# Four layers on one core: the last 96 GLU columns as a 192-column product with a DMA transpose, in place of key features paired by sign

## The chip, the cores and the metric

The kernel runs on one core of a Trainium2 chip. The metric is the device time of one execution in microseconds; three runs of the kernel before gave a median of 396.29 us (395.6 to 396.61). The core has five engines that run side by side, each through its own list of instructions in order: TensorE (PE: matmuls, with a separate weight load), VectorE (DVE), ScalarE (ACT), GpSimd (POOL) and SyncE (SP, which here only issues DMAs). Matmuls write to PSUM, eight banks of 128 partitions by 512 floats; everything else lives in SBUF, 128 partitions wide.

## The reference

The input is x, 2048 tokens by 512, in bf16. Four residual layers follow, A, B, A, B, with the same weights for both A and for both B:

```
x = x + A(layernorm(x));  x = x + B(layernorm(x));  twice

A: q, k, v = x @ wqkv                       # 32 heads of 16
   pq, pk  = q @ w_phi, k @ w_phi           # a 16x16 matrix for each head
   phi_q   = [softmax(pq), softmax(-pq)]    # 32 features for each head
   phi_k   = [softmax(pk), softmax(-pk)]
   kv = sum_s phi_k[s]^T v[s];  z = sum_s phi_k[s]
   o  = (phi_q kv) / (phi_q z + 1e-6);  return o @ wo

B: h = relu(x @ W_gate) * (x @ W_up)        # 512 -> 1376
   return h @ W_down                        # 1376 -> 512
```

A is linear attention: one pass over all tokens sums the 16 x 16 matrices kv of each head and sign, a second pass applies them. B is a gated unit whose inner width is 1376 = 10 x 128 + 96.

## The kernel before, in words

All weights and all activations stay in SBUF. The 2048 tokens are 16 tiles of 128, and four tiles make a slab of 512. `x_sb` holds tokens on partitions; after each layer norm (`ln`) the tile is transposed by a DMA (issued by SP, `dma_tr`, L393) into `yT`, with features on partitions, as the matmuls want it.

**Layer A, keys and values.** `kv_proj` (one tile) and `kv_pair` (two tiles) project a tile to pk and v in PSUM. w_phi is folded into the weights beforehand (`compose_k`, `compose_q`). ACT takes exp(pk) and exp(-pk) to `expk` and copies v to `vsb`, DVE sums each head's 16 features (`Zk`) and takes reciprocals (`rZk`), POOL multiplies (`phik`, L640; for the last two tiles half of it is DVE's). Then `kv_acc` (L662) adds the tile to the running sum in PSUM with eight matmuls, one for each of eight groups. In this version a group is four heads with both signs: 4 x 2 x 16 = 128 features as weights against 64 columns of v and one column of ones, 65 columns in all. The sums fill two banks, 0 and 1. When the last tile is in, `kv_fin` (L671) copies them to `kvbd`, masked so that each head keeps its own block, in two signs by two halves: four copies (L678) and four denominators (L683) on 64 partitions each, on DVE.

**Layer A, queries.** `q_proj` (L688) projects a slab and takes the exponentials (`expq`). `num` (L700) multiplies a tile's eight feature groups with `kvbd`: eight matmuls of 144 columns (L710), in three banks' worth of groups. Then come the normalization on DVE and POOL, a DMA transpose to `oT`, the product with wo (L741) and the residual (L743).

**Layer B.** `glu_up` (L747) goes through the 11 chunks of the inner width for a slab, or for a piece of two tiles (the first slab is cut into two such pieces). For each chunk it makes four matmuls for gate and four for up with the weights stationary and the slab's tokens as 512 (or 256) columns (L762), into two PSUM banks from a ring of four. ACT takes the relu of gate (L764); for the chunks in `on_act` ACT also copies up to a scratch in `expk` (L770) and DVE multiplies from SBUF (L772), otherwise DVE multiplies from PSUM (L775). The result, hidden units on partitions, goes to one of 18 units of `hT`. The last chunk is 96 wide and comes last. `glu_down` (L781) takes 11 matmuls for each tile (L790) and adds to x (L792).

**The order of work.** `emit` (L802) lists operations layer by layer, mixing the chunks of B with the numerators of the same layer pair and the keys of the next layer. Each operation carries a planned duration. `Program.schedule` then makes the order of each engine itself: it derives the dependences from the resources that each operation reads and writes (a PSUM bank, a tile, an hT unit), and searches by list scheduling forwards and backwards with the planned durations, keeping the order with the shortest planned span. So a changed duration or dependence can move any instruction. Within an engine the order is then fixed, waits included. In layer 0 the first slab's queries are projected early, through a ring of two banks, 2 and 3 (`qr0`, L811); bank 3 also serves `compose_q`.

## Time and profile before

| what | value |
|---|---|
| median of three runs | 396.29 us |
| profiled execution | 396.61 us, span 394.9 us |
| PE | 376.9 us busy (95% of the span), 2331 matmuls |
| DVE | 271.8 us busy (69%) |
| ACT | 205.7 us busy (52%) |
| POOL | 173.3 us busy (44%) |
| gate and up products (L762) | 880 matmuls, 259.0 us busy by the modelled ends |
| key-value accumulation (L666) | 256 matmuls of 65 columns, 12.7 us busy |
| granted PE clock, mean | 0.991 |

The span runs from the first to the last instruction of the program; the profiled execution's own time is 1.7 us longer. Busy time of PE is counted with modelled ends of the matmuls, which overlap in the pipeline, so a mean duration (193 ns for 65 columns, 379 ns for 512) says how long one takes from start to result, and not how far apart two of them start. In the view of slices each digit stands for one fortieth of the span, about 9.9 us, in tenths.

The stages in time: to about 56 us layer 0's keys and values, to about 75 us the first numerators of layer 0, to 225 us layers 0 and 1 mixed and the first keys of layer 2, to 246 us the rest of layer 2's keys and the accumulation, to 262 us its first numerators, and then layers 2 and 3 mixed, to the end.

### The profile page before, as it was taken

What the parts mean: (1) busy time and instruction counts of PE and PEld (TensorE: products, weight loads), DVE (VectorE), ACT (ScalarE), POOL (GpSimd) and SP (SyncE); (2) the same over time, 40 slices, a digit from 0 to 9 for tenths busy, and PEclk for the clock granted to TensorE, in tenths of its full rate; (3) what the DMA queues carried; (4) which work ended last, traced back from release to release, by engine and by line L of the source; (5) the groups of instructions that cost most, each with busy time, mean ns of one, the idle gap of its engine ahead of it and who ended that gap; (6) DMA issues with size and microseconds to landing.
All of it is one profiled execution on the core that took longest, in us unless ns stands there. A gap on an engine that the chain in (4) does not pass through costs nothing.

```text
span 394.9 us, 6391 instructions
## 1 busy us (share of the span) xinstructions
PE 376.9 (95%) x2331; PEld 202.0 (51%) x2331; DVE 271.8 (69%) x551; ACT 205.7 (52%) x389; POOL 173.3 (44%) x286
## 2 busy tenths in 40 slices
PE   5897979899999999999999998899999999999997
PEld 4443435576844544444444454457774454444444
DVE  4999677896756888867766856897886675422222
ACT  5987768743634303542354375985563652553340
POOL 6499833751633373364243643385464352100000
PEclk9999889999999999999999999999999999999999
DMA  6833681322311223300100020133232113100002
GB/s 191 224 62 48 180 316 27 68 53 42 54 27 40 42 41 68 69 12 15 27 13 2 13 42 2 27 72 69 49 68 55 40 28 80 28 14 13 17 24 66
DMA packets 61663, 23.01 MB, mean 58 GB/s; under 512 B 53472, under 2 KB 60608, under 8 KB 61632
## 3 DMA queue, kind: packets, MB, share of 16 engines
q1 hardware_dynamic: 60912, 22.02, 24.1%
q10 hardware_dynamic: 720, 0.59, 0.5%
q8 instruction: 18, 0.29, 0.3%
q14 instruction: 13, 0.11, 0.1%
HBM read 7.91 MB, written 2.10 MB: 25 GB/s over the span
## 4 chain that ended last, share of the span: by engine, by line
PE 80%; POOL 6%; DVE 6%; DMA 3%; issue 3%; ACT 1%; SPq 0%; POOLq 0%; DVEq 0%; ACTq 0%
PE ps L762 39%; PE ps L790 19%; PE ps L621 7%; PE ps L741 5%; PE ps L694 4%; PE ps L710 3%; DMA yT<-ytile 2%; PE ps L666 1%; DVE stats L555 1%; POOL rstd L563 1%; POOL osb L735 1%; PE ps L652 1%; POOL expk L640 1%; DMA x_sb<-in_A_x_dram 1%; DVE kvbd L678 1%
## 5 line engine op out<-in xcount | busy, mean ns | idle before, releaser
L762 PE MATMUL ps<-yT,Wg 128*128 128x512 bf16 (+3 forms) x440 | 129.9, 337 | 0.9 <-DMA yT<-ytile 0.9
L762 PE MATMUL ps<-yT,Wu 128*128 128x512 bf16 (+3 forms) x440 | 129.1, 337 | 0.0
L764 ACT ACTIVATE gate_sb<-ps 128x512 bf16<-128x512 f32 (+3 forms) x110 | 56.1, 513 | 113.5 <-PE ps L762 110.3
L790 PE MATMUL ps<-Wd,hT 128*128 128x512 bf16 (+2 forms) x363 | 103.1, 373 | 0.0
L640 POOL TENSOR_TENSOR expk<-expk,rZk 128x1024 bf16<-128x1024 bf16 (+1 forms) x32 | 59.1, 1863 | 38.0 <-DVE rZk L635 29.4
L762 PEld LDWEIGHTS ps<-yT,Wg 128*128 128x128 bf16 (+1 forms) x440 | 43.5, 100 | 35.0 <-issue 1.2
L762 PEld LDWEIGHTS ps<-yT,Wu 128*128 128x128 bf16 (+1 forms) x440 | 43.8, 100 | 32.8 <-ACT expk L770 0.2
L772 DVE TENSOR_TENSOR hT<-gate_sb,expk 128x512 bf16<-128x512 bf16 (+3 forms) x73 | 29.5, 407 | 38.8 <-ACT expk L770 29.7
L790 PEld LDWEIGHTS ps<-Wd,hT 128*128 128x128 bf16 (+1 forms) x363 | 35.2, 98 | 37.2 <-DVE x_sb L792 0.9
L555 DVE BATCH_NORM_STATS2 stats<-x_sb 128x6 f32<-128x512 bf16 x64 | 42.4, 681 | 4.9 <-DMA x_sb<-in_A_x_dram 4.4
L633 DVE TENSOR_REDUCE Zk<-expk 128x64 f32<-128x1024 bf16 x32 | 37.9, 1201 | 8.1 <-ACT expk L624 5.9
L735 POOL TENSOR_TENSOR osb<-tsc 128x512 bf16<-128x512 bf16 x28 | 33.5, 1199 | 15.5 <-DVE tsc L730 14.6
L367 ACT ACTIVATE numbf<-ps 128x432 bf16<-128x432 f32 x64 | 32.8, 538 | 13.6 <-PE ps L710 12.0
L741 PE MATMUL ps<-wo_p,oT 128*128 128x512 bf16 x128 | 38.8, 379 | 0.8 <-DMA oT<-osb 0.7
L710 PE MATMUL ps<-kvbd,expq 128*128 128x144 bf16 x256 | 33.9, 231 | 5.0 <-DVE kvbd L683 3.7
L770 ACT ACTIVATE expk<-ps 128x512 bf16<-128x512 f32 (+3 forms) x73 | 36.3, 498 | 1.1 <-PE ps L762 0.9
L694 PE MATMUL ps<-yT,Wqp 128*128 128x512 bf16 x128 | 36.5, 390 | 0.0
L697 ACT ACTIVATE expq<-ps 128x1024 bf16<-128x1024 f32 (+1 forms) x40 | 32.8, 861 | 7.0 <-PE ps L694 6.4
L562 POOL TENSOR_SCALAR rv<-mv 128x1 f32<-128x1 f32 (+1 forms) x53 | 13.2, 250 | 50.1 <-DVE mv L557 49.9
L792 DVE TENSOR_TENSOR x_sb<-x_sb,ps 128x512 bf16<-128x512 bf16 (+1 forms) x33 | 22.0, 668 | 18.9 <-PE ps L790 18.6
L624 ACT ACTIVATE expk<-ps 128x512 bf16<-128x512 f32 x44 | 23.9, 596 | 19.0 <-PE ps L621 18.7
L563 POOL TENSOR_TENSOR rstd<-rv,mhalf 128x1 f32<-128x1 f32 (+1 forms) x53 | 31.5, 596 | 3.5
(75 smaller groups left out, 429.0 us busy)
## 6 DMA issues: line engine op xcount, KB each, us to landing
out_dram<-x_sb SPq DMA_DIRECT2D x15, 128.0 KB, 1.7
x_sb<-in_A_x_dram SPq DMA_DIRECT2D x3, 512.0 KB, 6.1
Wu<-in_B_W_up_dram SPq DMA_DIRECT2D x4, 344.0 KB, 5.1
Wg<-in_B_W_gate_dram SPq DMA_DIRECT2D x4, 344.0 KB, 5.6
Wd<-in_B_W_down_dram SPq DMA_DIRECT2D x5, 256.0 KB, 7.6
yT<-ytile SPq DMA_TRANSPOSE x60, 2.5
hT<-in_A_wqkv_dram ACTq DMA_DIRECT2D x4, 128.0 KB, 3.0
x_sb<-in_A_x_dram SPq DMA_DIRECT2D x4, 128.0 KB, 3.6
```

The source lines that it names most:

```text
L555: op("dve", (lambda t: lambda e: e.bn_stats(k.stats6[:, t, :], k.x_sb[:, t, :]))(t), [r("x", t)], [r("st", t)], 685, f"{tag} stats {t}")
L563: op("pool", lambda e: e.tensor_tensor(k.rstd[:, t0:t1, :], k.rv1[:, t0:t1, :], k.mhalf[:, 0:n], ALU.pow), [r("rv1", t) for t in ts] + [r( ...
L633: op("dve", lambda e: e.tensor_reduce(k.Zk[:, zb, :], k.expk[:, t, :, :, :].rearrange("p g s (h f) -> p (g s h) f", f=16), AX.X, ALU.add), ...
L640: op(eng, (lambda kv, u0, n: lambda e: e.tensor_tensor(kv, kv, k.rZk[:, rb, u0 * 32:u0 * 32 + n].unsqueeze(2).to_broadcast([P, n, 16]), AL ...
L694: op("pe", (lambda c, ic, bank: lambda e: e.matmul(k.pb[bank][:], k.Wqp[:, ic, c * 128:(c + 1) * 128], k.yT[:, ic, st * 512:(st + 1) * 512 ...
L710: op("pe", (lambda s, c, j, g0, bank: lambda e: e.matmul(k.pb[bank][:, j * GW:(j + 1) * GW], k.expq[:, st, c, s, tt * 128:(tt + 1) * 128], ...
L735: op(sm, lambda e: e.tensor_tensor(k.osb[:, b, :], k.tsc[:, b, 0:512], k.tsc[:, b, 512:1024], ALU.add), [r("tsc", b)], [r("osb", b)], 418 ...
L741: op("pe", (lambda c, bank: lambda e: e.matmul(k.pb[bank][:], k.oT[:, ob, c, :], k.wo_p[:, c, :], start=(c == 0), stop=(c == NC - 1)))(c, ...
L762: op("pe", (lambda bank, W, ic, fc, Mf: lambda e: e.matmul(k.pb[bank][0:Mf, 0:n], W[:, ic, fc * 128:fc * 128 + Mf], k.yT[:, ic, c0:c0 + n] ...
L764: op("act", (lambda Mf, gb, gs: lambda e: e.activation(k.gate_sb[0:Mf, gs, 0:n], k.pb[gb][0:Mf, 0:n], ACT.Relu))(Mf, gb, gs), [self.RP[gb] ...
L770: op("act", (lambda Mf, ub, up: lambda e: e.activation(up[0:Mf, 0:n], k.pb[ub][0:Mf, 0:n], ACT.Copy))(Mf, ub, up), [self.RP[ub]], ru, 170 ...
L790: op("pe", (lambda fc, Kf, u, c0, bank, m0, m1: lambda e: e.matmul(k.pb[bank][:, m0:m1], k.hT[0:Kf, u, c0:c0 + 128], k.Wd[0:Kf, fc, m0:m1] ...
```

## The change

Two things are exchanged.

The pairing by sign goes. `expk` is laid out by sign and then by head, a group of `kv_acc` is now eight heads of one sign, 8 x 16 = 128 features, and its matmul runs over these eight heads' 128 columns of v and one column of ones: 129 columns. There are still eight matmuls for a tile. The sums now fill three banks (0, 1 and 2), so `qr0` keeps bank 3 alone. `kv_fin` makes three copies and three denominators on 128 partitions, one pair for each bank; a numerator product needs only the pair of its own three groups. `kvbd` is written in full by the masked copies and isn't zeroed any more.

The last 96 columns of gate and up become one product. `Wg` and `Wu` are now the two halves of one tile `Wgu`. For each token tile four matmuls with the tokens as weights and 2 x 96 = 192 columns leave gate and up side by side in PSUM, tokens on partitions, two tiles to a bank. ACT takes the relu of all tiles of the slab at once, DVE multiplies from PSUM into `h10t` (96 of 128 columns, the rest zeroed once by POOL), and a DMA transpose on SP brings it into the slab's `hT` unit. This step, `last`, stands first in each slab; the ten full chunks follow, and the down product still reads it as its last chunk. `last` has no variant with ACT's copy of up.

```diff
-        sb("Wg", [NC, F])
-        sb("Wu", [NC, F])
+        sb("Wgu", [NC, 2, F])
+        self.Wg, self.Wu = self.Wgu[:, :, 0, :], self.Wgu[:, :, 1, :]
-        sb("expk", [NT, NG, 2, 64])
-        sb("vsb", [NT, NG, 66])
+        sb("expk", [NT, 2, 512])
+        sb("vsb", [NT, NC, 130])
+        sb("h10t", [4, 128])
-        sb("mask4", [4])
...
-        op("pool", lambda e: e.memset(k.vsb[:, :, :, 64:66], 1.0), [], [r("vones")], 250, "v ones")
-        op("pool", lambda e: e.tensor_tensor(k.mask4[:], k.mask8[:, 0:4], k.mask8[:, 4:8], ALU.add), [r("mask8")], [r("mask4")], 150, "mask4")
-        op("pool", lambda e: e.memset(k.kvbd[:], 0.0), [], [r("kvones")] + [r("kvbd", s, u) for s in range(2) for u in range(2)], 1000, "kvbd zero")
+        op("pool", lambda e: e.memset(k.vsb[:, :, :, 128:130], 1.0), [], [r("vones")], 250, "v ones")
+        op("pool", lambda e: e.memset(k.h10t[:], 0.0), [], [r("h10t")], 900, "h10t zero")
...
     def kv_acc(self, t, tag):
         op, r, k = self.op, self.r, self
         for g in range(NG):
-            bank, col = g // 4, (g % 4 // 2) * 256 + (g % 2) * 66
-            op("pe", (lambda g, bank, col: lambda e: e.matmul(
-                k.pb[bank][:, col:col + 65], k.expk[:, t, g, :, :].rearrange("p s m -> p (s m)"), k.vsb[:, t, g, 0:65],
-                start=(t == 0 and g % 4 == 0), stop=(t == NT - 1), skip_group_check=True))(g, bank, col),
-               [r("phik", t, bank), r("v", t), r("vones")], [self.RP[bank]], KVD, f"{tag} kvacc {t} {g}")
+            s, c = g // 4, g % 4
+            bank, j = g // 3, g % 3
+            op("pe", (lambda s, c, bank, j: lambda e: e.matmul(
+                k.pb[bank][:, j * 130:j * 130 + 129], k.expk[:, t, s, c * 128:(c + 1) * 128], k.vsb[:, t, c, 0:129],
+                start=(t == 0 and j == 0), stop=(t == NT - 1), skip_group_check=True))(s, c, bank, j),
+               [r("phik", t, s), r("v", t), r("vones")], [self.RP[bank]], 59, f"{tag} kvacc {t} {g}")
...
     def kv_fin(self, tag):
         op, r, k = self.op, self.r, self
-        for s in range(2):
-            for u in range(2):
...
+        for bank in range(3):
+            g0 = bank * 3
+            n = min(3, NG - g0)
+            pv = k.pb[bank][:, 0:n * 130].rearrange("p (g m) -> p g m", m=130)
+            op("dve", (lambda g0, n, pv: lambda e: e.tensor_tensor(
+                k.kvbd[:, g0:g0 + n, 0:128].rearrange("p g (d h) -> p g d h", h=8),
+                pv[:, :, 0:128].rearrange("p g (h d) -> p g d h", h=8),
+                k.mask8[:].unsqueeze(1).unsqueeze(1).to_broadcast([P, n, 16, 8]), ALU.mult))(g0, n, pv),
+               [self.RP[bank], r("mask8")], [r("kvbd", bank)], 550 if n == 3 else 430, f"{tag} kvbd {bank}")
+            op("dve", (lambda g0, n, pv: lambda e: e.scalar_tensor_tensor(
+                k.kvbd[:, g0:g0 + n, 128:136], pv[:, :, 128:129].to_broadcast([P, n, 8]), 0.5 * EPS_DEN,
+                k.mask8[:].unsqueeze(1).to_broadcast([P, n, 8]), ALU.add, ALU.mult))(g0, n, pv),
+               [self.RP[bank], r("mask8"), r("kvbd", bank)], [r("kvbd", bank)], 200, f"{tag} kvden {bank}")
...
-                   [r("expq", st, c, s), r("kvbd", s, 0), r("kvbd", s, 1), r("kvones")], [self.RP[bank]], 63, f"{tag} num {t} {g0 + j}")
+                   [r("expq", st, c, s), r("kvbd", gb), r("kvones")], [self.RP[bank]], 63, f"{tag} num {t} {g0 + j}")
...
-            Mf = 128 if fc < 10 else FLAST
+            Mf = 128
...
+        def last():
+            fc, m = NFC - 1, len(ts)
+            b0, b1 = next(ring), next(ring)
+            pv = k.ps[:, b0:b0 + 2, :].rearrange("p b (c m) -> p (b c) m", c=2)
+            u = self.unit % NHU
+            self.unit += 1
+            gs = u % 3
+            for j, t in enumerate(ts):
+                self.unit_of[t, fc] = (u, j * 128)
+                for ic in range(NC):
+                    op("pe", (lambda t, j, ic: lambda e: e.matmul(pv[:, j, 0:2 * FLAST].rearrange("p (a f) -> p a f", a=2), k.yT[:, ic, t * 128:(t + 1) * 128], k.Wgu[:, ic, :, F - FLAST:F], start=(ic == 0 and j % 2 == 0), stop=(ic == NC - 1), skip_group_check=True))(t, j, ic),
+                       [r("Wg", ic), r("Wu", ic), r("yT", t)], [self.RP[(b0, b1)[j // 2]]], 84, f"{tag} gu {t} {fc} {ic}")
+            RB = [self.RP[b0], self.RP[b1]] if m > 2 else [self.RP[b0]]
+            gv = k.gate_sb[:, gs, 0:m * FLAST].rearrange("p (j f) -> p j f", j=m)
+            op("act", lambda e: e.activation(gv, pv[:, 0:m, 0:FLAST], ACT.Relu), RB, [r("gate", gs)], 170 + m * FLAST * 0.833, f"{tag} relu {ts[0]} {fc}")
+            op("dve", lambda e: e.tensor_tensor(k.h10t[:, 0:m, 0:FLAST], gv, pv[:, 0:m, FLAST:2 * FLAST], ALU.mult),
+               [r("gate", gs)] + RB, [r("h10t")], 150 + m * FLAST * 1.04, f"{tag} h {ts[0]} {fc}")
+            self.dma_tr(lambda e: e.dma_start_transpose(k.hT[:, u, 0:n].rearrange("p (j q) -> p j q", j=m), k.h10t[:, 0:m, :].rearrange("p j f -> p (j f)")),
+                        [r("h10t")], [r("hT", u)], f"{tag} htr {ts[0]}")
+
+        out.append(last)
-        for fc in range(NFC):
+        for fc in range(NFC - 1):
             out.append(lambda fc=fc: step(fc))
...
-        kr0, qr0 = cycle([4, 5, 6, 7]), cycle([2, 3])
+        kr0, qr0 = cycle([4, 5, 6, 7]), cycle([3])
```

The exponentials, the copy of v and `knorm` follow the new layout with the same sizes; where `phik` is split between POOL and DVE it is now split by sign.

## The prediction

> **What bounds the kernel now.** I read the page's slices first, then the chain, then stages in the view of windows, then the timeline of single instructions where a stage changes. The slices show TensorE (PE) full nearly everywhere and its granted clock dipping once:
>
> ```profile
> PE   5897979899999999999999998899999999999997
> PEclk9999889999999999999999999999999999999999
> ```
>
> The chain agrees: 80% of the span is PE, 38.7% on the gate and up products (L762), 1.3% on the key-value accumulation (L666).
>
> ```profile
> by line: PE ps L762 38.7%; PE ps L790 19.2%; PE ps L621 7.4%; PE ps L741 5.3%; PE ps L694 4.2%; PE ps L710 3.3%; issue 2.8%; DMA yT<-ytile 2.3%; PE ps L666 1.3%; DVE stats L555 1.2%; POOL rstd L563 1.1%; POOL osb L735 1.1%; PE ps L652 1.0%;
> ```
>
> By windows (columns: stage, its length, then busy time of PE, weight load, DVE, ACT, POOL), the GLU stages have PE at 73.9 of 75, 75 of 75, 67.5 of 68 and 52 of 52 us. There every column of a product is on the path. Only the first 75 us have PE idle worth the name:
>
> ```profile
> 24.00:40.00 16.00, 13.26 (x114) 6.75 (x113) 16.00 (x20) 11.75 (x15) 16.00 (x11) 1.00 0.40 62
> 40.00:56.00 16.00, 14.40 (x119) 7.05 (x119) 12.21 (x17) 11.19 (x19) 11.46 (x7) 0.89 0.79 263
> 150.00:225.00 75.00, 75.00 (x349) 34.36 (x348) 55.47 (x96) 30.65 (x55) 32.77 (x39) 1.00 0.14 26
> ```
>
> In 24 to 40 us DVE and POOL are full and PE waits; from 75 us on PE is the bound.
>
> A matmul's mean duration is latency, not pace. The pace comes from runs of one product in the timeline: (length minus one duration) / (count minus one).
>
> ```profile
> 228.44 0.62 PE L666 MATMUL ps<-vsb,expk 128*128 128x65 bf16 x15
> 67.00 0.54 PE L710 MATMUL ps<-kvbd,expq 128*128 128x144 bf16 x6
> 103.50 0.82 PE L762 MATMUL ps<-yT,Wg 128*128 128x256 bf16 x6
> 223.63 1.46 PE L790 MATMUL ps<-Wd,hT 128*128 128x512 bf16 x6
> ```
>
> With durations of 193, 226, 273 and 379 ns these give 30.5, 62.8, 109.4 and 216.2 ns for 65, 144, 256 and 512 columns: 0.41 ns a column. Each of these matmuls loads its own 128x128 weights, so the load is hidden even at 30 ns.
>
> **The change part by part.** *Key-value accumulation.* 256 matmuls grow from 65 to 129 columns. Between the rows for 65 and 144 columns, 129 cost 56.7 ns, so +26.2 ns each, 3.35 us for the 128 of each layer. In layer 2 all 128 lie in 225 to 243 us, where the chain is PE without a break: **+3.35**. In layer 0, 56 start before 40 us and 72 between 40 and 56. The 56 (1.47 us) I cost at nothing: PE idles 2.74 us in 24 to 40 while DVE and POOL are full; without that cover they cost 1.47. The 72 cost **+1.9**: PE runs without a gap from 40 to 53.5 us, and what they displace there is query projection that must then run later, where PE is full. Ends: 0 (the chain at 47 to 54 us is ACT, then DVE) and 1.9.
>
> The Trainium skill ("TensorE: Matmul & The Clock Gate", Back-to-back issue gap) gives about 81 ns for a 128-column matmul in a stream with weight loads, against 56 ns alone. That rule speaks against the change: by it the accumulation would cost 256 x (81 - 30.5) = 13 us, an estimate from the page. The 62.8 ns of 144 columns, in just such a stream, contradicts it.
>
> *Last 96 columns.* Before, a slab of four tiles takes 8 matmuls of 512 columns, 1730 ns; after, 16 of 192 columns at 62.8 + 48 x 0.416 = 82.8 ns, 1325 ns: -0.405 us for each of 6 slabs. The four pieces of two tiles take 8 x 109.4 = 875 ns before, 8 x 82.8 = 662 after: -0.213 each. Together **-3.28**, all in stages where PE is full. Ends: -3.28, and 0 if a 192-column product paced like one of 256.
>
> ACT loses eight copies of up (4 x 588 + 4 x 375 ns) and shorter relus; it waits 110 us for PE in L764, so this is worth nothing. DVE multiplies from PSUM over 384 elements (about 550 ns between the rows of 411 for 256 and 685 for 512) where it took 424: +0.13 us in slabs whose DVE has 19 of 75 us free: nothing, at most 0.5 if DVE were the bound.
>
> *The new transposes.* Ten DMA transposes join 92 on SP's queue, each 1.19 us there and 2.5 us to landing. Each waits for DVE's product, and behind it in SP's order stand the transposes of yT and oT; SP does wait long for DVE already, so it is not full. The result is read by the last matmul of a tile's down product, at least ten steps of 0.87 us (two tiles) later: 2.5 us is covered. Cost 0; ends 0 and +1.0, if a held yT arrives late at a slab's start. Its hT unit is freed by the last rather than the first matmul of the old slab's last down product, up to 10 x 0.216 = 2.2 us later; DVE already waits 8.2 us in four such places under a full PE, so nothing, and at most 2.2 without it. At the two first pieces PE waits 0.9 us for the second tile's yT; a product per tile can start with the first tile (0.33 us each): **-0.3**, ends 0 and -0.6.
>
> *End of the accumulation.* Here PE stands still for DVE:
>
> ```profile
> 242.26 0.41 PE L666 MATMUL ps<-vsb,expk 128*128 128x65 bf16 x8
> 242.74 1.32 DVE L678 TENSOR_TENSOR kvbd<-ps,mask 64x256 bf16<-64x256 f32 x3 [2.00 <-PE ps L666]
> 244.09 0.36 DVE L683 SCALAR_TENSOR_TENSOR kvbd<-ps,mask 64x16 bf16<-64x16 f32 x2
> 244.51 0.42 PE L710 MATMUL ps<-kvbd,expq 128*128 128x144 bf16 x4 [1.84 <-DVE kvbd L683]
> ```
>
> Three masked copies and two denominators run before the first numerator product. After, one copy of 384 elements (422 ns for 256, 684 for a 512-element add: about 553) and one denominator (171) suffice: 0.83 us with the gaps; if DVE again does all copies first, 553 + 553 + 422 + 171 and gaps, about 1.8. I take the middle, 1.3, since both orders are open: -0.5 in each layer, **-1.0**; ends 0 and -2.0.
>
> *One bank less.* The third accumulator bank leaves layer 0's first query projection bank 3 alone, shared with the composing of Wq. Three of its matmuls that ran at 21.8, 30.7 and 37.0 us move past 40 us: **+0.65** (3 x 0.216), ends 0 and 0.65. In each layer four matmuls of the next slab's projection (0.86 us) move behind the accumulator's release; the longer accumulation takes their place: 0, at most +0.86 each. With one bank each round waits for its two exponentials (0.86 + 1.2 + 0.2, four rounds 9.1 us) and there are 10 us from 44 to 54.
>
> *Setup.* POOL drops a memset of 1.06 us and a mask and adds one memset; PE there waits for the load of Wk (3.4 us): 0.
>
> Sum: 3.35 + 1.9 - 3.28 - 0.3 - 1.0 + 0.65 = **+1.3 us** on the profiled execution (span 394.9, 396.61 us with what lies around it, 0.32 above the median of 396.29). On the median: **397.6 us**.
>
> **The rivals.** *B, nothing covers the accumulation (slower).* For it: PE busy is 95% and the whole order of work is planned anew. PE's bare work is +6.7 - 3.28 = +3.4: 399.7 us; with both lost projections or a late transpose 401. Here belongs a 192-column product at the pace of 256 columns (+3.3 on the forecast, 400.9).
>
> *C, layer 0 covers all of it.* For it: the chain from 47 to 54 us is ACT and DVE. Against it: PE is full from 40 to 53.5. 1.3 - 1.9 = -0.6: 395.7.
>
> *D, the clock (faster).* In layer 0 PE's gaps before the first numerators (0.56, 1.39 and 0.45 us) are followed by half clock; the first column after POOL's is the granted clock:
>
> ```profile
> 57.00:58.00 1.00, 0.77 (x4) 0.50 (x5) 0.17 (x1) 0.67 (x2) 0.00 (x0) 0.59 0.89 273
> 58.00:59.00 1.00, 1.00 (x6) 0.45 (x5) 0.22 (x1) 0.22 (x1) 0.00 (x0) 0.50 0.08 26
> 59.00:60.00 1.00, 1.00 (x6) 0.62 (x5) 0.83 (x4) 0.01 (x1) 0.00 (x0) 0.50 0.00 0
> 60.00:61.00 1.00, 1.00 (x6) 0.59 (x5) 0.93 (x3) 0.75 (x2) 0.00 (x0) 0.70 0.00 0
> ```
>
> That costs 0.4 + 0.5 + 0.5 + 0.3 = about 1.7 us of PE. In layer 2 the single gap of 1.84 us left the clock at 1.00. So if the gaps of layer 0, 2.4 us together, fall below 1.84, the loss may go: with the short stall in both layers too (a further -1.0), 1.3 - 1.7 - 1.0 = -1.4: 394.9 us. Against it: my own gap, 2.4 - 0.5, is just on the edge. The same edge threatens layer 2, where a longer gap would add 1.7.
>
> The page named above ("Why this matters for your kernels") says that gaps under about 3 us leave the clock alone. The loss at 57 us after 2.4 us of gaps speaks against it; by the page D would be worth only its shorter stall, 396.6 us.
>
> **How the numbers follow.** 0.3% of this kernel is 1.2 us, about what a measurement can tell from no change: faster is below 395.1, slower above 397.5. The forecast, A, gets 0.40; its own range is 396.0 to 399.2, since the order of all work is planned anew from other durations and can gain or lose about what PE idles in one stage (1.6 us at 40 to 56); it splits 0.22 slower, 0.17 same, 0.01 faster. B has 0.24, all slower. C has 0.12: 0.08 same, 0.04 faster. D has 0.24: 0.19 faster, 0.05 same. Sums: faster 0.24, same 0.30, slower 0.46. The range reaches from beyond D's centre, at 394.0, to most of B, at 400.9.
>
> **What would show it.** In the changed profile: the 129-column product paced near 57 ns and the 192-column one near 83; PE busy up by about 3 us in all; PE without a gap from 225 to the end of layer 2's accumulation, some 3 us later than 242.7; its gap there near 1.3 us; a GLU slab of four tiles 0.4 us shorter; a granted clock below 1.00 still there behind layer 0's accumulation (if not, D); no wait of PE for a transpose of h. The prediction is wrong if PE turns out not to be full in the GLU stages after the change, or if the new plan moves the waits for yT near 38 us, where the clock falls to 0.53, which the diff does not touch.

## The result: 390.41 us against 395.95, faster

The kernel after took 390.41 us (median of four executions, 389.96 to 390.54); the kernel before, on the same chip, took 395.95 (394.68 to 396.61). The ratio is 0.9862, with a 95% interval from 0.9835 to 0.9889. The forecast was 397.6 us with a range of 394.0 to 400.9: both the sign and the range were wrong.

The profiled execution after took 390.43 us, with a span of 388.6; the one before 396.61 and 394.9. So 6.3 us of span are to be found between the two traces. One fact on the clock is needed for all that follows: 13 of the 19 executions of the kernel before beside the first experiments had a mean granted clock of 0.996 or less and took 395.9 us (median), the other six 394.1, while none of the 45 executions of the kernel after and of those made from it lost more than 0.001. So about 1.8 us of the 5.5 are clock, and some 3.7 remain at equal clock. That takes the clock's share from another chip; on the one chip where the clocks of both kernels are listed, three executions of before at clock 1.00 took 394.32 (median) and after 389.5, which is 4.8.

The slices of the page of after, to be read as those of before: each digit is a fortieth of the span, in tenths.

```profile
PE   4999989999999999999999999989999999999996
PEclk9999999999999999999999999999999999999999
```

The two 7s of PE in slices 4 and 6 of before are gone, and so are the two 8s of the clock in slices 5 and 6. The page gives PE 375.3 us busy, where it was 376.9 in a span 6.3 us longer.

Five marks divide the span: when the first numerator matmul (the line with `kvbd` and `expq`) starts in layers 0 and 2, and when the first gate-and-up matmul starts in layers 1 and 3.

| from the timeline, us | before | before's order at full clock | after | stage, after - before | stage, after - full clock |
|---|---|---|---|---|---|
| first numerator, layer 0 | 56.35 | 54.64 | 53.42 | -2.93 | -1.22 |
| first gate and up, layer 1 | 76.39 | 73.14 | 70.81 | -2.65 | -1.11 |
| first numerator, layer 2 | 244.51 | 241.65 | 238.23 | -0.70 | -1.09 |
| first gate and up, layer 3 | 263.34 | 260.98 | 255.32 | -1.74 | -2.24 |
| end of the span | 394.9 | 392.5 | 388.6 | +1.72 | +1.76 |

Between the two profiled kernels nearly all of the gain lies in the first 76 us, where the forecast had a loss, and in layers 2 and 3 a gain of 1.74 is given back by the end. But the profiled execution of before ran at half clock from 40.11 to 43.52 us and from 57.18 to 60.59. The column "full clock" is the trace of an experiment below: the kernel before, its order of work unchanged, with 42 matmuls of one column ahead, in an execution that kept its clock. Against it 2.3 of 3.9 us lie in the first 76.

**Where the first 2.93 us come from.** The next two fences show POOL's row of key multiplications in layer 0 (`phik`; columns: start, length, instruction, how often, and in brackets the idle time before it and who ended it). First the timeline of POOL before:

```profile
28.01 17.11 POOL L640 TENSOR_TENSOR expk<-expk,rZk 128x1024 bf16<-128x1024 bf16 x9
46.72 3.82 POOL L640 TENSOR_TENSOR expk<-expk,rZk 128x1024 bf16<-128x1024 bf16 x2 [1.59 <-ACT expq L697]
50.98 2.52 POOL L640 TENSOR_TENSOR expk<-expk,rZk 128x512 bf16<-128x512 bf16 x2 [0.45 <-ACT expq L697]
```

And the timeline of POOL after:

```profile
25.97 25.75 POOL L636 TENSOR_TENSOR expk<-expk,rZk 128x1024 bf16<-128x1024 bf16 x14
```

Before, the row ended at 53.50, after 2.04 us in which POOL had nothing to multiply. After, fourteen of them (the last two are halves of 128x512, merged into the row) run without a break and end at 51.72, 1.78 us earlier. From there to the first numerator it is 2.85 us before (53.50 to 56.35) and 1.70 after (51.72 to 53.42): another 1.15. The sum is the 2.93.

The first of the two parts is not the change's. The timelines of POOL and PE in before's order at full clock:

```profile
27.97 20.89 POOL L640 TENSOR_TENSOR expk<-expk,rZk 128x1024 bf16<-128x1024 bf16 x11
49.25 2.52 POOL L640 TENSOR_TENSOR expk<-expk,rZk 128x512 bf16<-128x512 bf16 x2 [0.40 <-ACT expq L697]
...
54.64 0.42 PE L710 MATMUL ps<-kvbd,expq 128*128 128x144 bf16 x4 [1.40 <-DVE kvbd L683]
```

There the row ends at 51.77, as in after, and the first numerator follows at 54.64. So the 1.78 us go with the late transpose and the half clock at 40 us, which the diff doesn't touch. What stays is the tail behind POOL's row, 2.87 us there and 1.70 in after. The timelines show two pieces of it. Before, the last accumulation waits until 54.10 for DVE's half of the last tile's multiplication, 0.6 us longer than for POOL; after, DVE's halves are done at 50.82. And before, DVE needs 1.77 us (54.58 to 56.35) for three copies and two denominators ahead of the first numerator; after, two copies and a denominator take 1.15 (52.25 to 53.40). Neither piece was tried apart.

**The end of the accumulation.** In layer 2 PE stood still for 1.84 us before. The timeline after, PE's lines and then DVE's:

```profile
235.35 2.82 PE L665 MATMUL ps<-vsb,expk 128*128 128x129 bf16 x46
238.01 0.38 PE L692 MATMUL ps<-yT,Wqp 128*128 128x512 bf16 x1
238.23 0.54 PE L708 MATMUL ps<-kvbd,expq 128*128 128x144 bf16 x6
...
236.89 1.07 DVE L676 TENSOR_TENSOR kvbd<-ps,mask 128x384 bf16<-128x384 f32 x2 [1.43 <-PE ps L665]
237.88 0.30 DVE L681 SCALAR_TENSOR_TENSOR kvbd<-ps,mask 128x24 bf16<-128x24 f32 x2
238.21 0.42 DVE L676 TENSOR_TENSOR kvbd<-ps,mask 128x256 bf16<-128x256 f32 x1
```

DVE begins to copy at 236.89, while PE still has about 1 us of accumulation for the other banks: the new plan finishes one bank after the other, and each copy waits for its own bank alone. When the last accumulation is issued, two of the three copies are made, and the numerators follow without a gap. Layer 0 shows the same (copies from 52.25, accumulation to 52.8, numerators at 53.42).

The windows of both kernels around layer 2's accumulation and first numerators (stage, length, busy time of PE, weight load, DVE, ACT, POOL, then clock, share and rate of DMA). Before:

```profile
226.20:244.50 18.30, 16.47 (x185) 9.49 (x183) 12.02 (x21) 13.14 (x23) 8.43 (x8) 1.00 0.11 22
244.50:263.30 18.80, 17.27 (x118) 9.09 (x118) 15.54 (x40) 16.04 (x24) 9.41 (x21) 1.00 0.21 43
```

And after:

```profile
222.00:238.20 16.20, 16.20 (x170) 11.39 (x169) 11.80 (x19) 9.66 (x18) 7.62 (x6) 1.00 0.09 18
238.20:255.30 17.10, 16.89 (x116) 9.26 (x116) 14.21 (x37) 15.02 (x23) 8.65 (x18) 1.00 0.23 46
```

PE had 1.83 and 1.53 us free in the two stages before, and has 0 and 0.21 after. 47 query matmuls now run behind the first numerators, where it was 40; they fill what was idle there.

**Where 1.72 us are given back.** The chain of waits after (start, length, what), and in the next fence the timeline of PE after at the same place:

```profile
253.44 4.44 DMA yT<-ytile
```

```profile
257.93 0.51 PE L785 MATMUL ps<-Wgu,yT 128*128 128x192 bf16 x4 [1.69 <-DMA yT<-ytile]
```

At layer 3's first piece the product of the second tile waits for that tile's `yT`. Its transpose took 4.44 us from issue to landing; the median of the 60 transposes of that line is 2.4. Two kernels below in which this wait is absent take 131.49 and 131.43 us for the last stage, against 131.54 before, so the wait accounts for the 1.72. What the product saves in that stage is hidden in part, since eight numerator matmuls and two with wo (0.9 us by their paces) stand behind the mark after that stood ahead of it before.

**Paces.** From the runs above and `70.81 0.49` for four matmuls of 192 columns, with durations of 220 and 246 ns in the groups: 129 columns take (2.82 - 0.22) / 45 = 57.8 ns, 192 columns (0.49 - 0.246) / 3 = 81 ns. The forecast had 56.7 and 82.8.

### The profile page after: what moved, and what is told of

It is laid out like the page before. It is cut to its first block, busy times and chain, and to the rows that moved or that the text cites. A ratio compares the mean times of both kernels' runs of the same rounds, so it can differ in the third digit from the quotient of the medians.

```text
span 388.6 us, 6472 instructions
## 1 busy us (share of the span) xinstructions
PE 375.3 (97%) x2379; PEld 209.0 (54%) x2379; DVE 271.4 (70%) x547; ACT 201.4 (52%) x381; POOL 169.1 (44%) x285
## 4 chain that ended last, share of the span: by engine, by line
PE 86%; POOL 4%; ACT 4%; DMA 3%; DVE 2%; issue 1%; SPq 0%; DVEq 0%; POOLq 0%
PE ps L760 35%; PE ps L808 19%; PE ps L619 7%; PE ps L739 6%; PE ps L692 5%; PE ps L650 4%; PE ps L708 4%; PE ps L665 3%; PE ps L785 3%; POOL expk L636 1%; DMA yT<-ytile 1%; DMA x_sb<-in_A_x_dram 1%; DMA oT<-osb 1%; ACT expk L622 1%; POOL rstd L561 1%; DVE stats L553 1%
## 5 line engine op out<-in xcount | busy, mean ns | idle before, releaser
L760 PE MATMUL ps<-yT,Wgu 128*128 128x512 bf16 (+1 forms) x800 | 177.9, 337 | 0.0
L760 PEld LDWEIGHTS ps<-yT,Wgu 128*128 128x128 bf16 x800 | 76.9, 98 | 60.6 <-ACT expk L767 1.2
L808 PE MATMUL ps<-Wd,hT 128*128 128x512 bf16 (+2 forms) x363 | 105.8, 373 | 0.0
L762 ACT ACTIVATE gate_sb<-ps 128x512 bf16<-128x512 f32 (+1 forms) x100 | 50.8, 513 | 82.6 <-PE ps L760 67.6
L769 DVE TENSOR_TENSOR hT<-gate_sb,expk 128x512 bf16<-128x512 bf16 (+1 forms) x65 | 28.2, 435 | 29.4 <-ACT expk L767 24.6
L739 PE MATMUL ps<-wo_p,oT 128*128 128x512 bf16 x128 | 40.1, 379 | 0.3 <-DMA oT<-osb 0.3
L692 PE MATMUL ps<-yT,Wqp 128*128 128x512 bf16 x128 | 34.8, 379 | 0.7 <-ACT expq L695 0.6
L767 ACT ACTIVATE expk<-ps 128x512 bf16<-128x512 f32 (+1 forms) x65 | 32.4, 499 | 1.4 <-PE ps L760 1.2
L596 DVE TENSOR_SCALAR ytile<-x_sb,mv,rstd 128x512 bf16<-128x512 bf16 x52 | 23.1, 447 | 12.0 <-POOL rstd L561 11.5
L772 DVE TENSOR_TENSOR hT<-gate_sb,ps 128x512 bf16<-128x512 bf16 (+1 forms) x35 | 21.3, 609 | 13.3 <-PE ps L760 10.5
```

The costliest lines, as they stand in the source:

```text
L692: op("pe", (lambda c, ic, bank: lambda e: e.matmul(k.pb[bank][:], k.Wqp[:, ic, c * 128:(c + 1) * 128], k.yT[:, ic, st * 512:(st + 1) * 512 ...
L739: op("pe", (lambda c, bank: lambda e: e.matmul(k.pb[bank][:], k.oT[:, ob, c, :], k.wo_p[:, c, :], start=(c == 0), stop=(c == NC - 1)))(c, ...
L760: op("pe", (lambda bank, W, ic, fc, Mf: lambda e: e.matmul(k.pb[bank][0:Mf, 0:n], W[:, ic, fc * 128:fc * 128 + Mf], k.yT[:, ic, c0:c0 + n] ...
L762: op("act", (lambda Mf, gb, gs: lambda e: e.activation(k.gate_sb[0:Mf, gs, 0:n], k.pb[gb][0:Mf, 0:n], ACT.Relu))(Mf, gb, gs), [self.RP[gb] ...
L808: op("pe", (lambda fc, Kf, u, c0, bank, m0, m1: lambda e: e.matmul(k.pb[bank][:, m0:m1], k.hT[0:Kf, u, c0:c0 + 128], k.Wd[0:Kf, fc, m0:m1] ...
```

## The experiments

All times are medians; "before" is the kernel before on the same chip.

| kernel | us | before | ratio, 95% interval |
|---|---|---|---|
| only the 192-column product | 394.47 | 395.77 | 0.9976 (0.9948 to 1.0004) |
| only the keys unpaired | 391.61 | 395.77 | 0.9901 (0.9881 to 0.9920) |
| after, every copy waits for all banks | 392.37 | 395.77 | 0.9919 (0.9898 to 0.9939) |
| before, yT wait taken out | 393.57 | 395.77 | 0.9967 (0.9945 to 0.9988) |
| after, 65 columns accumulated | 389.70 | 395.11 | 0.9861 (0.9834 to 0.9888) |
| after, 1.5 us more on POOL | 391.45 | 395.72 | 0.9894 (0.9871 to 0.9917) |
| after, 1.73 us more on PE | 389.27 | 395.72 | 0.9837 (0.9814 to 0.9860) |
| after, fetches moved by 4 matmuls | 389.10 | 395.11 | 0.9844 (0.9812 to 0.9875) |
| after, fetches moved by 52 | 388.93 | 395.11 | 0.9842 (0.9816 to 0.9868) |
| after, fetches moved by 96 | 389.30 | 396.04 | 0.9839 (0.9806 to 0.9872) |
| after, again | 389.50 | 396.04 | 0.9851 (0.9820 to 0.9882) |
| before, fetches moved by 42 | 395.22 | 395.11 | 1.0003 (0.9982 to 1.0024) |

The kernel after took 390.41 us on its first chip and 389.5 on another, with the kernel before at 396.04 there. Differences of less than 1 us between chips are therefore not read. Its two traces also have the first numerator of layer 0 at 53.42 and at 52.72; POOL's row of fourteen starts at 25.97 and at 25.27, so that from the row's start it is 27.45 us in both. Where less than 1 us matters in layer 0, it is counted from there.

### Each half alone

The kernel before with the product alone (keys still paired):

```diff
-        sb("Wg", [NC, F])
-        sb("Wu", [NC, F])
+        sb("Wgu", [NC, 2, F])
+        sb("h10t", [4, 128])
...
+        out.append(last)
-        for fc in range(NFC):
+        for fc in range(NFC - 1):
```

> The kernel before with only the 192-column product and its transpose; keys stay paired. Theory 1 (the gain of the whole change comes from the un-pairing: copies out of three separate banks and an earlier tile 12 in layer 0): here only the bare matmul saving of 3.3 us, so 392 to 393 us, with PE's stall of 1.8 us before the first numerators still there in both layers, the wait for yT near 38 us and both stretches of half clock. Theory 2 (the 192-column product brings the gain): 390 us or less.

The kernel after with the old last chunk, so that only the keys are changed:

```diff
-            Mf = 128
+            Mf = 128 if fc < 10 else FLAST
...
-        out.append(last)
-        for fc in range(NFC - 1):
+        for fc in range(NFC):
```

> The changed kernel with the old last chunk of gate and up; keys un-paired. Theory 1: bare matmul +6.7 us, stalls before the numerators -3.7, their half clock -1.7, wait for yT and its half clock -4.3: about 393 us, and a granted clock of 1.00 throughout. Theory 2: the longer accumulation costs about what it is longer by, less what layer 0 hides: 398 to 402 us.

The product alone gave 394.47, unpairing alone 391.61, both 390.41 (on another chip). So unpairing is worth about 4.2 us, and the product about 1.2 on top of it; on the paired base its 1.3 us are not told from nothing, as the interval includes 1. Both theories were off for the product, which was to give 3 us or more, and unpairing, which the forecast had as the part that costs, is the part that gains. At equal clock the split is sharper: the executions at clock 1.00 are 394.13 before, 394.14 with the product alone and 391.61 with unpairing alone, all on one chip, and 390.4 after. So at equal clock unpairing gives 2.5 us, and the product alone nothing. Each of these kernels has a plan of its own, and what comes from the edit and what from the new plan is not told apart by the times.

The markers show where. In the trace of unpairing alone, the time from the first numerator of layer 0 to that of layer 2 is 239.49 - 53.13 = 186.36 us, and from there to the end 150.41. In after it is 184.81 and 150.37. The product gains 1.55 in layer 1, close to its half of the forecast, and nothing in layer 3, where the wait for `yT` stands.

### The copies by bank

The kernel after, but every copy waits for all three banks, as it did before:

```diff
-               [self.RP[bank], r("mask8")], [r("kvbd", bank)], ...
+               [self.RP[0], self.RP[1], self.RP[2], r("mask8")], [r("kvbd", bank)], ...
```

> The changed kernel, but each masked copy waits for all three accumulator banks, as the copies of the kernel before waited for both of theirs. Theory 1: PE stands still before the first numerators in each layer, 1.0 to 1.8 us each, 392.5 to 394 us, and up to 1.7 more if the clock falls behind the stall of layer 0. Rival (the stalls went for another reason, or are filled by query products): within 0.5 us of 390.4.

It took 392.37, 1.96 us more than after on its first chip: 0.1 short of the theory's 392.5 to 394, and the rival's 390.4 within 0.5 falls. Layer 2 in its timeline, PE and then DVE:

```profile
236.36 1.99 PE L665 MATMUL ps<-vsb,expk 128*128 128x129 bf16 x32
238.19 1.02 PE L692 MATMUL ps<-yT,Wqp 128*128 128x512 bf16 x4
239.55 0.55 PE L708 MATMUL ps<-kvbd,expq 128*128 128x144 bf16 x6 [0.34 <-DVE kvbd L681]
...
238.38 1.02 DVE L676 TENSOR_TENSOR kvbd<-ps,mask 128x384 bf16<-128x384 f32 x2 [2.71 <-PE ps L665]
```

DVE now starts its copies at 238.38, only after PE's last accumulation, 1.5 us later than in after; the plan puts four query matmuls there, and PE still waits 0.34. From the end of POOL's last multiplication (236.58) to the numerators it is 2.97 us, against 1.86 in after (236.37 to 238.23) and 2.85 before. So in layer 2 the wait for one bank alone brings the whole of that shortening. In layer 0 it doesn't: there this kernel's first numerator starts at 53.48, against 53.42. It loses 0.70 more behind that, in the numerators (first gate and up at 71.57 against 70.81). By its marks it loses 0.76 us to layer 1's first gate and up, 0.56 more to layer 2's first numerator, and 0.4 behind that, where no copy stands; so some 1.3 of its 1.7 us of span lie where the copies are, and the rest is the plan, which was made anew.

### What sets layer 0

The columns first. The kernel after with 65 columns in the accumulation of tiles 1 to 15, its order of work unchanged:

```diff
-   k.pb[bank][:, j * 130:j * 130 + 129], ..., k.vsb[:, t, c, 0:129],
+   k.pb[bank][:, j * 130:j * 130 + (129 if t == 0 else 65)], ..., k.vsb[:, t, c, 0:(129 if t == 0 else 65)],
```

> The changed kernel with the accumulation of tiles 1 to 15 cut to 65 columns (half of v's columns and the column of ones left out of the sums there), in the same order of work: the price of the 64 columns alone, 240 x 26.2 ns = 6.3 us of PE. Theory P (my prediction: what PE does in layer 2, and behind 40 us in layer 0, is on the path): 5 us faster, about 385.3. Theory Q (PE's extra work takes the place of idle time, as the stages behind each accumulation are bound by DVE, POOL and transposes): 1 to 3 us faster, 387.5 to 389.5.

Half of v's columns and the column of ones are left out of the sums of these tiles. It took 389.70, against 389.10 of the kernel after with four small matmuls ahead (below) on the same chip: 6.6 us of PE's work (240 x 27.3 ns, from the paces of 57.8 and 30.5) are gone and no time is, so that even the smaller of the two expected gains is missed. The first numerator of layer 0 comes 27.36 us after the start of POOL's row, where it is 27.45 in after. PE waits instead, in the timeline of this kernel in layers 0 and 2:

```profile
49.26 0.35 PE L665 MATMUL ps<-vsb,expk 128*128 128x65 bf16 x6 [0.87 <-POOL expk L636]
50.81 0.25 PE L665 MATMUL ps<-vsb,expk 128*128 128x65 bf16 x3 [0.77 <-POOL expk L636]
...
236.07 0.94 PE L665 MATMUL ps<-vsb,expk 128*128 128x65 bf16 x26 [1.13 <-POOL expk L636]
```

The releaser is POOL's `phik` each time. In layer 2 the stage from the first accumulation to the first numerator is 14.82 us against 15.33 in after: 0.5 us for 3.3 us of columns.

So POOL's row, not PE, should be what sets layer 0. Two kernels test it directly. The first gives POOL three memsets of 0.5 us ahead of tile 8's multiplication, the second gives PE eight matmuls more just where its trace showed no gap (both edits shortened):

```diff
 a) knorm, tile 8 of layer 0, ahead of the multiplication on POOL
+   [e.memset(k.gate_sb[:, i, :], 0.0) for i in range(3)]
 b) kv_pair, tiles 6 to 9 of layer 0: the first of four products twice
-   e.matmul(..., start=(ic == 0), stop=(ic == NC - 1))
+   e.matmul(..., start=True, stop=True); e.matmul(..., start=True, stop=False)   # ic == 0
```

> The kernel after with three memsets of 128x512 on POOL (0.53 us each, into the gate scratch, which layer 0 does not use) ahead of the multiplication of tile 8 in layer 0; the order of work is the same. POOL gets 1.5 us more to do in its row of 14 multiplications (25.97 to 51.72 us, without a gap). Theory G (layer 0 is set by POOL's row of key multiplications, and TensorE only follows): the last multiplication ends 1.5 us later, the first numerator starts at about 55.0 instead of 53.4, and the time is 1.1 to 1.6 us above the kernel after (389.5 to 390.4 on two chips). Rival (TensorE sets layer 0, as the prediction had it): below 0.4 us.

> The kernel after with eight matmuls of 512 columns more on TensorE in layer 0: the first of the four products of k and v is done twice for tiles 6 to 9 (the second overwrites the first), 8 x 216 ns = 1.73 us, in 33 to 40 us, where TensorE had no gap in the trace of after; the order of work is the same. Theory G (POOL sets layer 0): the first numerator starts within 0.4 us of 53.4 and the time is within 0.5 us of the kernel after. Rival (TensorE sets layer 0): the first numerator 1.4 to 1.7 us later and the time 1.2 to 1.7 us above the kernel after.

With 1.45 us more on POOL: 391.45 us, first numerator at 55.08. With 1.73 us more on PE: 389.27, first numerator at 53.68. The timeline of the first:

```profile
26.26 11.47 POOL L636 TENSOR_TENSOR expk<-expk,rZk 128x1024 bf16<-128x1024 bf16 x6
37.66 1.45 POOL L636 MEMSET gate_sb<- 128x512 bf16 x3
39.08 14.32 POOL L636 TENSOR_TENSOR expk<-expk,rZk 128x1024 bf16<-128x1024 bf16 x8
...
55.08 0.55 PE L708 MATMUL ps<-kvbd,expq 128*128 128x144 bf16 x6
```

and of the second:

```profile
25.81 25.86 POOL L636 TENSOR_TENSOR expk<-expk,rZk 128x1024 bf16<-128x1024 bf16 x14
53.68 0.54 PE L708 MATMUL ps<-kvbd,expq 128*128 128x144 bf16 x6
```

POOL's row ends 1.7 us later in the first, 0.3 of which it starts later, and the numerators move by the same 1.66; in the second it ends at 51.67, as in after. Counted from the row's start the first numerator comes 1.37 us later in the first kernel and 0.42 in the second. Theory G holds on both, its rival on neither; that the second's time stays at 389.27 owes something to luck in layer 3 (below), and the numerator is the better measure. Its window shows how a full PE can mislead:

```profile
40.00:54.00 14.00, 13.98 (x127) 8.83 (x126) 11.58 (x18) 9.89 (x17) 11.61 (x7) 1.00 0.75 233
```

Busy for 13.98 of 14 us, and yet most of the 1.73 us cost nothing: between the start of POOL's row and the first numerator PE had 0.89 us of gaps in after, and has 0.02 here. There is no more room, so a further load on PE would show.

### The wait at 40 us and the clock

In the trace of before PE waits 2.17 us until 39.97 for a transpose, and its clock is halved from 40.11 to 43.52. In after that wait is not there; DVE makes tile 12's layer norm at 31.1 instead of 34.1. The kernel before with that order alone:

```diff
-           [r("expk", t, 0), r("expk", t, 1)], [r("Zk", zb)], ...
+           [r("expk", t, 0), r("expk", t, 1)] + ([r("yt", 0)] if tag == "A0" and t == 6 else []), [r("Zk", zb)], ...
```

> The kernel before, with one dependence more: in layer 0 the sums of tile 6's keys on DVE come after the normalized tile 12, so that its transpose starts some 4 us earlier. Theory 1: PE's gap of 2.2 us near 38 us and the half clock behind it (1.7 us) go: about 392 us. Rival (what follows is bound by DVE and POOL in any case, so the gap only moves): 395 to 396.5 us.

393.57, 1.3 us below before by the ratio, with an interval from 0.5 to 2.2: a part of the 3.8 us that theory 1 expected, and more than its rival allowed. The gap at 40 is gone and one of 0.40 us has come at 44; POOL's row is dry for 1.07 us at another place and ends at 53.49, as before. The stall ahead of the numerators is as it was (1.39 and 0.45). In the profiled execution the clock stays at 1.00, but six of its ten executions lose 0.004 to 0.005 of it, hardly fewer than the 13 of 19 of the kernel before. So this order takes the wait at 40 us away, and neither POOL's dry places nor, for most executions, the loss of the clock.

### A transpose that meets an instruction fetch

The transposes that land late have something in common. The traces show DMAs of 16 KB of instructions on queue 8, 18 times for the 4662 matmuls and weight loads in before and 19 for 4758 in after: a fetch for about each 250 of them. Leaving out the loads of the first 10 us, 14 transposes in the two traces took 3.9 us or more to land, and each of them had such a fetch in its flight, 1.0 to 2.5 us after its issue. Matmuls of one column, into a bank not yet in use, ahead of all of PE's work move every fetch (two PE instructions each, with the weight load):

```diff
+   ...
+   for _ in range(52):    # 4, 42, 96 in the others
+       eng.matmul(self.pb[7][:, 0:1], self.ident[:], self.ident[:, 0:1], start=True, stop=True)
    prog.emit_engine(name, eng, sems, dsems)
```

> The changed kernel with 52 one-column matmuls more at the start, while PE waits for its first load, in a corner of a bank that is written over later; the order of all else is the same. In the traces every transpose that took 4 us or more to land instead of 2.4 has a transfer of instructions on queue 8 in its flight, and those come at every 256th PE instruction (each matmul is two). 104 instructions more move the one at 255.9 us, which meets the yT transpose of layer 3's second tile, to about 247.8, where no transpose flies. Theory F (the fetch delays the transpose): that transpose lands after 2.4 us, PE's wait of 1.85 us at 257.9 goes, about 389 us. Rival (the delay comes from the transposes themselves, queued closely): 390 to 390.8 us, and the same transpose lands late again.

> The control to the run with 52: only 4 matmuls more, so that the fetch moves by 8 instructions, to about 255.4 us, still in the flight of the same transpose. Theory F: the late landing and the wait at about 258 us stay, 390.4 us within 0.5. If the mere presence of matmuls at the start (an earlier clock, say) brings something, it shows here.

> The kernel before with 42 one-column matmuls at the start, 84 PE instructions, which move the fetch at 36.9 us to about 32.1, out of the flight of the yT transpose that PE waits for at 40.0 us. Theory F: that transpose lands after 2.4 us, PE's gap of 2.3 us shrinks to about 0.7, the half clock behind it goes; what DVE and POOL bound stays, so 394.0 to 395.5 us. Rival (the late tile 12 on DVE alone makes the gap): gap and time unchanged, 395.5 to 396 us.

> 96 one-column matmuls on an unused bank are put ahead of the kernel after, in TensorE's idle start; nothing else differs. They move every instruction fetch of TensorE (one each 256 of its instructions) by 192 instructions: the fetches of layer 2 and 3 should stand near 241 and 260 us and miss the transposes of yT issued between 250 and 256 us. Theory F (a fetch in flight makes a transpose land late, and that is why TensorE waits 1.85 us near 258 us): the yT transpose near 253.4 us lands after 2.5 us, the gap of 1.85 us near 258 us is gone, no new wait for wo near 248 us comes in (that came in with 52 matmuls), and the time is 1.3 to 1.9 us below the kernel after on the same chip. Rival (the late transpose comes from the queue or from the layer norm, whatever the fetches do): the gap is still there, and the time is within 0.6 us of the kernel after on the same chip.

> The kernel after itself, as the base for the two shifted kernels. If the shift by 4 matmuls did nothing and its 389.1 us were the chip's, this runs below 390 us on a chip where the kernel before takes 395.1; if the 4 matmuls themselves gained, it runs at 390.4. The granted clock stays 1.00 and the gap of 1.85 us near 258 us is there.

With 4 matmuls the fetch stays at 255.51, and the `yT` transpose issued at 253.12 still lands after 4.40 us. With 52 it moves to 245.94: the same transpose, issued at 253.31, lands after 2.49, and the wait ahead of the second 192-column product is gone. But the fetch now meets the transpose of `oT` issued at 243.90, which lands after 4.10, and PE waits for that one. The timeline of PE with 52:

```profile
248.05 0.60 PE L739 MATMUL ps<-wo_p,oT 128*128 128x512 bf16 x2 [1.02 <-DMA oT<-osb]
...
256.30 0.49 PE L785 MATMUL ps<-Wgu,yT 128*128 128x192 bf16 x4
```

The view of DMA of the same kernel, in the window in which `yT` lands on time (253.3 to 255.9) and then in that of the late `oT` (244 to 248), has a line of queue 8 in the second alone (3.3 is the median of two transposes, of which one landed after 4.10):

```profile
yT<-ytile SPq DMA_TRANSPOSE x1, 2.5
...
q8 instruction: 1, 0.02, 1.5%
oT<-osb SPq DMA_TRANSPOSE x2, 3.3
```

With 96 the fetches stand at 240.12 and 259.71. The `yT` transposes near 253 land after 2.5 us, and the gap at 258 is gone, as expected; yet the fetch at 259.71 meets an `oT` transpose issued at 257.71 (4.08 us), and a wait of 0.97 us comes at 262.1, in the timeline of PE of that kernel:

```profile
262.06 0.60 PE L760 MATMUL ps<-yT,Wgu 128*128 128x256 bf16 x4 [0.97 <-ACT numbf L366]
```

The releaser that the line names is not the one: the transposed `oT` landed at 261.79, and the record of its product with wo, which stands here in the order of after (one matmul, 0.22 us), is missing from this trace; only its weight load, at 261.84, is there.

So the mechanism holds in each of the three: where the fetch goes, the late landing goes. The gain doesn't. 389.1 with 4, 388.93 with 52 (same chip), 389.3 with 96 and 389.5 for after itself (same chip) are the same within what can be measured, since with 52 and 96 a wait comes back at another transpose that has little slack. The 389 us that theory F expected with 52 is therefore no sign for it: the control with 4 has it too, 1.3 below what was expected of it. In after's second trace the clock is 1.00, the `yT` transpose lands after 4.04 us and the gap is 1.28. On the kernel before, 42 matmuls left 0.48 of the 2.17 us wait at 40 us and a wait of 1.42 came at 44; the time stayed at 395.22 against 395.11, and half of the executions still lost clock. The forecast gain of 1.3 to 1.9 us for 96 was wrong.

The kernel with 1.73 us more of PE work is the lucky case: its eight matmuls move the fetch to 252.94, where it meets a transpose of `oT` that is needed late. PE waits only 0.17 us for it, and from the first numerator of layer 2 to the end it takes 149.0 us against 150.37 in after. That is 1.4 us, about what the product should have gained in layer 3.

## Why the prediction was wrong, by its own steps

At equal clock the change is worth about -3.7 us (-4.8 on the chip where both kernels' clocks are listed) where the sum said +1.3.

**"In layer 0 the 72 cost +1.9": wrong, 0.** This is the step that turned the sign in layer 0. It rested on "PE runs without a gap from 40 to 53.5 us", which is true (13.5 of 13.5 us busy) and isn't what bounds. Of those, 3.4 us ran at half clock, and 19 matmuls (4.1 us) were query projection that can wait. What ends layer 0's key pass is POOL's row of multiplications, and the prediction's own windows showed POOL busy for 11.46 us of the 16 from 40 to 56, without asking when its row ended. The columns cost nothing (65 of them: the numerators 0.09 us earlier from the start of POOL's row), more PE work hardly anything (0.42 us for 1.73), while 1.45 us on POOL cost 1.37. Rival C had the size of this term right; it named ACT and DVE where the runs show POOL.

**"In layer 2 all 128 lie in 225 to 243 us: +3.35": size right for PE, wrong for the time, about 0.5.** The pace was right (57.8 ns against 56.7). But PE's full stage held query projection, of which the new plan moved seven matmuls (1.5 us) behind the numerators, where PE had idled. With 65 columns PE waits 1.13 us for POOL instead.

**"End of the accumulation: -1.0", with the middle between two orders: wrong, it was the far end, -2.0.** The prediction assumed that copies start when all accumulation ends, as in the trace of before, and asked only how many copies go first. It left out that once a copy waits for one bank, the plan can finish the banks one after the other and copy the first two under the accumulation of the last. PE's stall ahead of the numerators is 0 in both layers. Making the copies wait for all banks again costs 1.96 us, some 1.3 of it where the copies stand.

**"One bank less: +0.65" and up to +0.86 a layer: no such cost to be seen.** The displaced query matmuls run behind the numerators. The term wasn't tried by itself.

**"Last 96 columns: -3.28", and "-0.3" at the slab's start: -1.2 on the unpaired base, nothing at equal clock on the paired one.** The pace was right (81 ns against 82.8), and layer 1 gives 1.55 of its 1.79. In layer 3 the term "a held yT arrives late at a slab's start", which was kept as an end of the range under the new transposes, is what happened: 1.69 us. The cause named there (SP held by the new transposes) is not it; a fetch met a transpose of `yT`, and it would have met another with 52 or 96 matmuls more ahead. No engine waits for the transposes of `h10t` in the trace of after, so the cost of 0 for them holds.

**Rival D, the clock.** Its sign, and its half that the loss goes, held: the clock is 1.00 in every execution. It had the loss depend on the stall ahead of the numerators alone. That isn't the whole: a first half-clock stretch stands at 40 us, behind the wait for `yT`, which the prediction mentioned only in its list of what could make it wrong. With that wait alone gone, six of ten executions still lose clock; with stalls of 0.78 and 0.34 us ahead of the numerators of layers 0 and 2 and that wait gone (the copies behind all banks), none of four does. So the loss doesn't need the wait at 40 us. Whether the stall ahead of the numerators alone carries it stays open, since no run took that stall alone away.

**What the terms leave.** The sum of what the runs show apart is: columns about +0.5, copies by bank -2.0, product -1.2, which is -2.7 of -3.7 at equal clock. About the remaining 1.0 stands in layer 0, where the tail behind POOL's row is 1.15 us shorter although the copies' wait isn't what shortened it there (1.78 us with the copies behind all banks, 1.70 in after). The two pieces that the timelines show, DVE's half that is done earlier and its shorter copies, were not separated. That POOL's row no longer runs dry adds nothing to these: before's order has that too with the fetches moved by 42, and its executions at full clock take 394.27 us, against 394.6 for before's own on that chip.

The prediction named its own way to be wrong, that "the new plan moves the waits for yT near 38 us". That was part of it. It gave it no term and no chance. Nothing in the diff asks for it: that the new plan took this wait away is luck of the planning, and with it a part of the gain.

Two rules of the Trainium skill were weighed. "TensorE: Matmul & The Clock Gate", section "Back-to-back issue gap", has about 81 ns for a 128-column matmul in a stream with weight loads; the 46 matmuls of 129 columns above are 57.8 ns apart, so here the rule didn't hold. The page's rule of no idle gaps over about 3 us ("Why this matters for your kernels"), read so that shorter gaps leave the clock alone, didn't hold either: in the trace of before the clock is halved from 40.11 us, behind a gap of 2.17 us.

## What to carry to other kernels

A PE that is busy in every microsecond of a stage isn't by that alone its bound: ask for the row that ends the stage, here POOL's multiplications, and whether what fills PE could run later, where PE idles. A wait for one buffer instead of all was worth more here than the copies it saves, since a planner can then finish the buffers one by one and hide the copies under the rest. And where a whole order is planned anew, the waits that the diff doesn't touch are part of the change: list the waits of the old trace with no slack, and give their going a term and a chance.

## What the runs showed of the hardware

**Instruction fetches delay DMA transposes.** In the traces of before and after most transposes of 128 x 512 land 2.4 to 2.5 us after their issue, some after up to 3.4 with no fetch in flight. All 14 that took 3.9 to 4.6 us had a fetch of 16 KB on queue 8 between 1.0 and 2.5 us after their issue; five more with a fetch in flight took 2.9 to 3.7. Moving the fetch moved the late landing, in three kernels. The number of PE instructions ahead of a point thus helps to decide which transpose is late there, and a kernel that is longer by eight matmuls can be 1.4 us faster behind such a point.

**Half clock comes in stretches of 3.41 us.** In before they are 40.11 to 43.52 and 57.18 to 60.59, five times 3.41 apart; in the profiled execution of the product alone one begins at 57.35 and one at 262.15, sixty times 3.41 apart, and the second lasts 6.83. The window of that kernel there:

```profile
264.00:266.00 2.00, 2.00 (x15) 1.65 (x13) 1.52 (x5) 0.86 (x2) 0.58 (x3) 0.50 0.54 109
```

The Trainium skill ("TensorE: Matmul & The Clock Gate", section "What's actually happening") gives a free-running window of 3413 ns, which agrees. Each stretch of 3.41 us costs half of that, 1.7 us, of PE. That the same kernel loses the clock in some executions and not in others would fit a window whose phase differs from one execution to the next; no run here shows that by itself.
